# An attention-and-mixer kernel on one core: all work recast as jobs placed by a list scheduler

## The chip, the cores and the metric

The kernel runs on one core of a Trainium2 chip. Its engines are TensorE (PE in the rows, its weight loads PEld), VectorE (DVE), ScalarE (ACT), GpSimd (POOL) and SyncE (SP, which here only issues DMAs). The metric is the device time of one execution, in microseconds (us); lower is better.

## The reference, cut to what matters

The input x has 2048 tokens of 448 features. Two blocks follow each other, both on a normalised input:

```python
h  = x + A(layernorm(x))          # A: attention, 16 heads of 28
h2 = h + B(layernorm(h))          # B: gated mixer over the tokens
# A: qkv = xn @ wqkv; a token attends to the 8 tokens at distances 0, 2, .., 14 behind it
#    logits = q . k * scale; softmax over the 8; o = attn @ v; o @ wo
# B: z = gelu_tanh(hn @ w_in)                 (2048 x 1792)
#    z1 = z[:, :896];  z2 = layernorm(z[:, 896:])
#    g = w_sp @ z2 + b_sp[:, None]            (w_sp is 2048 x 2048)
#    B = (z1 * g) @ w_out
```

## The kernel before, in words

Everything is recorded through `iss`, which puts an instruction into the list of one engine and works out the semaphores that it must wait for. Each engine runs its list in order, and the order is the one in which the code below calls `iss`.

Tokens lie in 16 blocks of 128 (index m). The features, 448, are cut into 4 chunks of 112 rows (`DC`, `NCH`), so a product over the features is 4 matmuls. First x is loaded in four DMAs, with the weights and 16 transposing loads of the upper half of w_sp behind them in SP's list. Layer norm 1: `bn_stats` and `bn_aggr` for each block, one chain of small instructions for the inverse root (`rsqrt_chain`), one `tensor_scalar` for each block (L351). TensorE transposes the normalised block (L360) and VectorE copies it out into `xhT` (L369). Q and K come in tiles of 512 tokens (L383), V for each attention block (L400).

Attention runs in 18 blocks of 114 queries and 128 keys (`NQ`, `PAD`): 16 logit matmuls of 32 rows each, four of which can lie side by side in the array (L416), into banks 0 to 3 of the result memory; four exponentials (L423); one multiplication with the mask of the allowed distances (L432); 16 small matmuls with V, where the weights are the exponentials (L444); a reciprocal and a scaling (L454, L457); a transposition on TensorE (L472) and its copy (L475). `y_block` multiplies with wo and adds x (L485, L488), and L491 takes the squares for layer norm 2. One loop over the slots interleaves these by hand, with the Q, K tiles of later tokens as fillers.

Then the mixer. All layer norm 2 work comes first (16 norms, 64 transpositions). A pipelined loop over 32 half blocks makes z2 (L744). Gelu is built by hand in `GeluTile`: a copy on ScalarE (L708), three products on VectorE (L712 to L714), a sigmoid on ScalarE (L718), a product with a running sum on VectorE (L723), and squares on ScalarE (L733). When all 16 blocks have their sums, L787 normalises z2. The last loop runs over 28 tiles of 128 mixer columns by 512 tokens: 4 matmuls of z1 (L755) and its Gelu, 16 matmuls of w_sp with z2 (L800), bias and gate on VectorE (L813, L815); behind each 7 tiles come 4 blocks of the output product, 7 matmuls each (L823), the residual (L827) and the store (L829).

## Time and profile before

| | |
|---|---|
| time, three runs | 342.18, 343.89, 343.75 us; median 343.75 |
| profiled execution: first to last instruction | 342.4 us |
| mean granted TensorE clock | 0.915 of full speed |
| TensorE busy | 287.6 us (84%), 1859 matmuls |
| VectorE busy | 242.8 us (71%), 670 instructions |
| ScalarE busy | 156.8 us (46%), 320 instructions |
| GpSimd busy | 5.1 us (1%), 17 instructions |
| DMA | 16.39 MB, 40537 packets |

The profile has a time of its own only as the span, 342.4 us; 1.35 us lie between it and the median of the runs. Busy times say how much an engine did, not what the time waited for: that is read from the chain of waits and from the stretches (windows) of the span. A clock of 0.50 means 1.2 GHz, 1.00 means 2.4 GHz.

### The profile page before, as it was taken

To read this page: it belongs to the slowest core of one execution; us is meant where nothing else is said; L and a number is where in the kernel's file an instruction comes from. 1 tells how busy PE (TensorE), PEld (TensorE's weight loads), DVE (VectorE), ACT (ScalarE), POOL (GpSimd) and SP (SyncE) were. 2 spreads that over 40 slices of the span, in tenths; PEclk is the share of its full clock that TensorE was granted. 3 is DMA by queue.
4 is the path that set the end of the run, shared out by engine and by line. 5 is a ranking of instruction groups with operands and counts; after the bars stand their busy time and mean duration, and the time that the engine had idled before them with its cause. 6 is when DMAs were issued, how large, how long until landed. Compare 5 with 4: busy or idle time off the path is not lost.

```text
span 342.4 us, 4998 instructions
## 1 busy us (share of the span) xinstructions
PE 287.6 (84%) x1859; PEld 144.9 (42%) x1872; DVE 242.8 (71%) x670; ACT 156.8 (46%) x320; POOL 5.1 (1%) x17
## 2 busy tenths in 40 slices
PE   3789899999998848966550099999999999999996
PEld 1434455555565617521110034444444444444442
DVE  4987446897779779899999896554555565545554
ACT  1435878777866020899999322221222022212220
POOL 5000000000000000000000000000000000000000
PEclk9879989999987556999996589999999999999999
DMA  7999900000000069930000000001000100000001
GB/s 223 258 220 179 190 16 2 2 0 2 3 2 1 2 162 187 161 76 0 0 1 1 0 2 0 0 2 50 3 3 0 38 17 0 0 26 30 1 0 54
DMA packets 40537, 16.39 MB, mean 48 GB/s; under 512 B 34177, under 2 KB 39617, under 8 KB 40514
## 3 DMA queue, kind: packets, MB, share of 16 engines
q1 hardware_dynamic: 40514, 16.08, 22.5%
q8 instruction: 14, 0.23, 0.3%
q14 instruction: 9, 0.07, 0.1%
HBM read 5.85 MB, written 1.84 MB: 22 GB/s over the span
## 4 chain that ended last, share of the span: by engine, by line
PE 66%; DVE 28%; ACT 2%; issue 2%; DMA 1%; ACTq 0%; DVEq 0%
PE psum L800 29%; PE psum L383 9%; PE psum L755 7%; PE psum L823 6%; DVE z2p L723 5%; PE psum L400 4%; PE psum L485 4%; PE psum L444 4%; DVE wk L714 3%; DVE wk L712 3%; DVE wk L713 3%; DVE xhT L369 2%; DVE tring L351 2%; PE psum L416 2%; DVE st L347 1%
## 5 line engine op out<-in xcount | busy, mean ns | idle before, releaser
L708 ACT ACTIVATE xb<-psum 128x448 bf16<-128x448 f32 (+1 forms) x60 | 33.4, 558 | 108.3 <-PE psum L755 95.5
L800 PE MATMUL psum<-wspT_lo,z2p 128*128 128x512 bf16 x217 | 52.7, 388 | 17.9 <-DVE z2p L787 17.4
L712 DVE TENSOR_TENSOR wk<-xb 128x448 bf16<-128x448 bf16 (+1 forms) x60 | 24.2, 404 | 40.1 <-ACT xb L708 40.1
L800 PE MATMUL psum<-wspT_hi,z2p 128*128 128x512 bf16 x218 | 49.7, 379 | 0.3
L423 ACT ACTIVATE E<-psum 128x456 bf16<-128x456 f32 (+1 forms) x72 | 39.6, 550 | 15.1 <-PE psum L472 8.8
L800 PEld LDWEIGHTS psum<-wspT_lo,z2p 128*128 128x128 bf16 x224 | 21.9, 98 | 46.9 <-DVE z2p L787 22.3
L718 ACT ACTIVATE tb<-wk 128x448 bf16<-128x448 bf16 (+1 forms) x60 | 35.9, 598 | 12.7 <-DVE wk L714 12.7
L744 PE MATMUL psum<-w_in,xhT 112*128 112x448 bf16 x128 | 28.7, 365 | 11.1 <-ACT xb L708 11.1
L800 PEld LDWEIGHTS psum<-wspT_hi,z2p 128*128 128x128 bf16 x224 | 21.9, 98 | 26.5
L755 PE MATMUL psum<-xhT,w_in 112*128 112x512 bf16 x112 | 28.8, 379 | 1.2 <-ACT xb L708 1.2
L714 DVE TENSOR_TENSOR wk<-wk,xb 128x448 bf16<-128x448 bf16 (+1 forms) x60 | 24.5, 408 | 2.1
L744 PEld LDWEIGHTS psum<-w_in,xhT 112*128 112x128 bf16 x128 | 11.4, 101 | 28.0 <-ACT xb L708 19.0
L444 PEld LDWEIGHTS psum<-V,E 128*114 128x114 bf16 (+1 forms) x288 | 21.4, 149 | 2.4 <-issue 0.4
L823 PE MATMUL psum<-w_out,z1p 128*128 128x448 bf16 x112 | 22.0, 353 | 0.1
L444 PE MATMUL psum<-V,E 128*114 128x29 bf16 (+1 forms) x288 | 21.7, 210 | 0.0
L485 PE MATMUL psum<-wo,OT 112*128 112x448 bf16 x64 | 18.4, 420 | 3.9 <-DVE OT L475 2.8
L432 DVE TENSOR_TENSOR E<-E,maskb 128x1824 bf16<-128x1824 bf16 (+1 forms) x18 | 19.9, 1103 | 1.8 <-ACT E L423 1.7
L813 DVE TENSOR_TENSOR ub<-psum,bb 128x512 bf16<-128x512 f32 x28 | 19.1, 683 | 2.3 <-PE psum L800 2.3
L723 DVE CUSTOM_DVE_ANT_0 z2p<-tb,xb 128x448 bf16<-128x448 bf16 x32 | 19.8, 618 | 0.9 <-ACT tb L718 0.8
L383 PE MATMUL psum<-xhT,wqp 112*128 112x512 bf16 x64 | 18.1, 440 | 2.3 <-DVE xhT L369 2.3
L827 DVE TENSOR_TENSOR tring<-psum,x_tm 128x448 bf16<-128x448 f32 x16 | 10.0, 624 | 13.5 <-PE psum L823 13.5
L713 DVE TENSOR_SCALAR wk<-wk 128x448 bf16<-128x448 bf16 (+1 forms) x60 | 17.1, 285 | 2.1
(82 smaller groups left out, 338.1 us busy)
## 6 DMA issues: line engine op xcount, KB each, us to landing
x_tm<-in_A_x_dram SPq DMA_DIRECT2D x4, 448.0 KB, 7.2
out_dram<-tring SPq DMA_DIRECT2D x16, 112.0 KB, 1.7
w_in<-in_B_w_in_dram SPq DMA_DIRECT2D x1, 1568.0 KB, 15.5
stg<-in_A_wqkv_dram SPq DMA_DIRECT2D x1, 1176.0 KB, 9.9
w_out<-in_B_w_out_dram SPq DMA_DIRECT2D x1, 784.0 KB, 4.5
...
wspT_lo<-in_B_w_sp_dram SPq DMA_TRANSPOSE x16, 4.0
wspT_hi<-in_B_w_sp_dram SPq DMA_TRANSPOSE x16, 4.1
```

Of the source, the lines that this page charges most:

```text
L383: e.matmul(out_ap, wsrc[:, c, gg, :], xhT[0:DC, c, col0:col0 + 512], start=(c == 0), stop=(c == NCH - 1)),
L423: iss("act", lambda e, in_ap=in_ap, out_e=out_e: e.activation(out_e, in_ap, AF.Exp, scale=SCALE), reads=[r_bank[hh]], writes=[r_E[slot]])
L444: e.matmul(psum[0:nq, ob + h * 32: ob + h * 32 + DH + 1], E[0:nk, slot, eidx, 0:nq], V1[0:nk, vslot, h, 0:DH + 1]),
L708: iss("act", lambda e: e.activation(self.XB, self.in_ps_ap, AF.Copy), reads=[self.rbank], writes=[r_xb[s]])
L712: iss("dve", lambda e: e.tensor_tensor(self.WK, self.XB, self.XB, ALU.mult), reads=[r_xb[s]], writes=[r_wk[s]])
L714: iss("dve", lambda e: e.tensor_tensor(self.WK, self.WK, self.XB, ALU.mult), reads=[r_wk[s], r_xb[s]], writes=[r_wk[s]])
L718: iss("act", lambda e: e.activation(self.TB, self.WK, AF.Sigmoid, scale=GELU_K2), reads=[r_wk[s]], writes=[r_tb[s]])
L723: iss("dve", lambda e: e.tensor_tensor_reduce(self.out_dst_ap, self.TB, self.XB, 1.0, 0.0, ALU.mult, ALU.add, self.sum_x_ap), reads=[r_tb[ ...
L744: iss("pe", lambda e, c=c: e.matmul(out_ap, xhT[0:DC, c, PAD + 128 * m: PAD + 128 * m + 128], w_in[:, c, FH + D * k: FH + D * (k + 1)], st ...
L755: iss("pe", lambda e, c=c: e.matmul(out_ap, w_in[:, c, fc * 128:(fc + 1) * 128], xhT[0:DC, c, PAD + 512 * tc: PAD + 512 * (tc + 1)], start ...
L800: iss("pe", lambda e, sbk=sbk: e.matmul(out_ap, z2p[:, sbk, fc * 128:(fc + 1) * 128], wsrc[:, sbk, coff:coff + 512], start=(sbk == 0), sto ...
L823: iss("pe", lambda e, fc=fc: e.matmul(out_ap, z1p[:, fc, 128 * m:128 * m + 128], w_out[:, fc, :], start=(fc == 0), stop=(fc == FC7 - 1)), ...
```

## The change

The program is written again. Every piece of work is a `job`: an engine, a key (its rank), a duration written into the source, the instructions, the tiles that it reads and writes, and the banks of the result memory that it takes or gives back. `Planner.order` puts the jobs into one order: of the jobs whose inputs are ready on an engine it takes the lowest key, and one that is ready at once goes before one that is not. Then `Sched.issue` records them with their semaphores as before. What is different in the work:

- Chunks of the features are 128, 128, 128 and 64 rows. The rest of 64 rows is stored twice, in partitions 0 to 63 and 64 to 127, and two matmuls of 64 rows stand behind each other on the two halves of the array. So two tiles take 6 + 2 matmuls in place of 8.
- Two neighbouring banks are taken together, and one instruction empties both: Q and K of one group, two attention blocks of V, half of the heads' exponentials, both halves of z2, two tiles of z1, two blocks of y.
- Attention has 19 blocks of 112 queries; the exponentials as weights are 128 columns wide (they overlap the next head's).
- The transpositions of the normalised blocks 4 to 15, of the 19 attention outputs and of the 16 norms of h are DMAs from SBUF to SBUF (`dma_T`, 47 in all). Blocks 0 to 3 still go through TensorE. GpSimd copies the last 64 columns, so that the transposition also makes the second copy of the rest.
- The normalised blocks go through a ring of 6 (`xn`, `NR`), the attention outputs through one of 3 (`otm`, `NO`).
- The inverse roots are taken for two blocks at a time, 8 instructions on VectorE for blocks 0 to 3, 10 on GpSimd for all others.
- Gelu is one ScalarE instruction. The layer norms of h and of z2 use `bn_stats`, block by block, so there is no barrier over all blocks.
- b_sp is loaded already broadcast, 128 copies of 4 KB. The mixer's first product starts when the last logits are done (`gate`), z2 before z1 before g.

The core of the difference:

```diff
-NQ = 114
-PAD = 14
-NAB = 18
+NQ = 112
+KEYS = 128
+PAD = 16
+NAB = 19
+NPT = 4
+DMA_RATE = 0.25
+NWARM = 30
+FIRST = [(0, 2), (2, 4), "q", "v", (4, 8), (8, 12), (12, 16), "o"]
...
-        class GeluTile:
...
-                iss("dve", lambda e: e.tensor_tensor(self.WK, self.XB, self.XB, ALU.mult), reads=[r_xb[s]], writes=[r_wk[s]])
-                iss("dve", lambda e: e.tensor_scalar(self.WK, self.WK, GELU_C, 1.0, ALU.mult, ALU.add), reads=[r_wk[s]], writes=[r_wk[s]])
-                iss("dve", lambda e: e.tensor_tensor(self.WK, self.WK, self.XB, ALU.mult), reads=[r_wk[s], r_xb[s]], writes=[r_wk[s]])
...
-                iss("act", lambda e: e.activation(self.TB, self.WK, AF.Sigmoid, scale=GELU_K2), reads=[r_wk[s]], writes=[r_tb[s]])
...
-                    iss("dve", lambda e: e.tensor_tensor_reduce(self.out_dst_ap, self.TB, self.XB, 1.0, 0.0, ALU.mult, ALU.add,
-                                                               self.sum_x_ap),
...
-                iss("act", lambda e: e.activation(junk2[:, 0:self.n], self.out_dst_ap, AF.Square, accum_out=self.sum_sq_ap),
...
-        def ot_block(b):
...
-                iss("pe", lambda e, c=c: e.transpose(psb[0:DC, base + c * 128: base + c * 128 + nq],
-                                                    otm[0:nq, oslot, c * DC:(c + 1) * DC], ident[0:nq, 0:nq]),
...
+    def order(self):
...
+                    late = t > te[e] + 1e-9
+                    k = (late, t if late else 0, j.key, j.idx)
+                    if bestj is None or k < bestj[0]:
+                        bestj = (k, j, t, bk)
+                if bestj is not None and (cand is None or bestj[2] < cand[2]):
...
+        NR = 6
+        xn = sb("xn", [128, NR, 512], BF16)
+        NO = 3
+        otm = sb("otm", [128, NO, 512], BF16)
...
+        for what in FIRST:
+            if what == "v":
+                load_c("wv", wv, A_wqkv[:, 2 * D:3 * D], D, W_v)
+            elif what == "q":
+                load_c("wq", wraw, A_wqkv[:, 0:2 * D], 2 * D, W_qk)
+            elif what == "o":
+                load_c("wo", wo, A_wo, D, r_wo2)
+            else:
+                load_x(*what)
+        load_c("w_in", w_in, B_w_in, 2 * FH, r_wi, key=1.0)
+        load("bb", lambda: bb[:], lambda: B_b_sp.rearrange("(o n) -> o n", o=1).to_broadcast([128, S_TOK]), [r_bb], 0.48, 0, key=1.05, mb=0.5)
...
+        def ln_norm(k, m, mv, src3, rsrc, key, dup):
+            s = ringc[0] % NR
+            ringc[0] += 1
+            mu, rstd = mv[:, m, 0:1], rs[k][:, 3, m:m + 1]
+            pl.job("n%d_%d" % (k, m), "dve", key,
+                   [(lambda e: e.tensor_scalar(xn[:, s, 0:D], src3[:, m, :], mu, rstd, ALU.subtract, ALU.mult),
+                     [rsrc, r_mv[k][m], r_rs[k][m]], [r_xn[s]])], dve_t(D, 4, 2))
+            if dup:
+                pl.job("nd%d_%d" % (k, m), "pool", key,
+                       [(lambda e: e.tensor_copy(xn[:, s, D:512], xn[:, s, 384:D]), [r_xn[s]], [r_xnd[s]])], 0.34)
+            return s
+
...
+        def dma_T(name, dst, src, reads, writes, key):
+            return load(name, dst, src, writes, 1.15, 1.5, key=key, transpose=True, reads=reads)
...
+                def f(e, lo=lo, hi=hi, n=n, g=g, tk=tk):
+                    for k in range(2):
+                        for c in range(3):
+                            e.matmul(psv(tk, k, n), wap(0, 128, c, 2 * g + k), xhT[:, c, PAD + lo:PAD + hi],
+                                     start=(c == 0), stop=False)
+                    for k in range(2):
+                        ins = e.matmul(psv(tk, k, n), wap(64 * k, 64, 3, 2 * g + k),
+                                       xhT[64 * k:64 * k + 64, 3, PAD + lo:PAD + hi],
+                                       start=False, stop=True, tile_position=(64 * k, 0))
+                    return ins
+                pl.job("qk%d_%d" % (t, g), "pe", key, [(f, r_pad[2 * g:2 * g + 2] + xh_res(lo, hi), [])], pe_t(*([n] * 7)) + 0.1, acq=tk)
...
+                lgs[(b, j)] = pl.job("lg%d_%d" % (b, j), "pe", b + 0.0, [(f, rq, [])], 0.24, acq=tk, after=[o_jobs.get(b - NE)])
...
+            dma_T("oT%d" % b, lambda t0=t0, nq=nq: OT[:, :, t0:t0 + nq], lambda os=os, nq=nq: otm[0:nq, os, :],
+                  [r_otm[os], r_otd[os]], [r_OT[b]], b + 1.0)
...
+        gate = [lgs[(NAB - 1, 1)]]
...
+            pl.job("z2_%d" % m, "pe", ZK + m, [(f, r_wi + [r_hn[m]], [])], pe_t(*([D] * 7)) + 0.1, acq=tk, after=gate)
+            pl.job("z2g%d" % m, "act", ZK + m,
+                   [(lambda e, m=m, tk=tk: e.activation(
+                       z2p[:, m, :].rearrange("p (k n) -> p k n", k=2),
+                       psum[:, tk.b * 512:tk.b * 512 + 1024].rearrange("p (k n) -> p k n", k=2)[:, :, 0:D],
...
+            load("wlo%d" % s, lambda dst=dst, s=s: dst[:, s % 8, :], lambda s=s: B_w_sp[0:1024, 128 * s:128 * s + 128],
+                 [r_wlo[s]], 1.24, 1.9, key=3.0 + 1.0 * s, transpose=True)
...
+                    pl.job("g%d_%d_%d" % (fc, tc, q), "pe", GK + gi + 0.01 * q, [(f, rw + [r_z2[s] for s in ss], [])],
+                           pe_t(*([512] * 4)), acq=tk if q == 0 else None, use=[tk], reserve=4 if gi < 7 else 0)
...
+                pl.job("ua%d_%d" % (fc, tc), "dve", GK + gi,
+                       [(lambda e, tc=tc, s=s, tk=tk: e.scalar_tensor_tensor(ub[:, s, :], psv(tk), 1.0 / 16.0, bb[:, 512 * tc:512 * tc + 512], ALU.mult, ALU.add),
+                         [r_bb], [r_ub[s]])], dve_t(512), use=[tk], rel=tk)
...
```

SP's list from its start, in the kernel before. `stg` is wqkv, `wspT_lo` the transposed upper half of w_sp:

```order
L296 DMA x_tm<-in_A_x_dram 128x4x448 x2
L302 DMA stg<-in_A_wqkv_dram 112x4x1344
L296 DMA x_tm<-in_A_x_dram 128x4x448 x2
L305 DMA wo<-in_A_wo_dram 112x4x448
L306 DMA w_in<-in_B_w_in_dram 112x4x1792
L307 DMA bsp<-in_B_b_sp_dram 1x2048
L309 DMA_TRANSPOSE wspT_lo<-in_B_w_sp_dram 128x1024 x16
L666 DMA w_out<-in_B_w_out_dram 128x7x448
```

And in the changed kernel, from the load of w_in on. `wsp_la` is the first half of the same, `xhT` takes the transposed norms of x, `OT` the attention outputs; a wait names the engine, and none on these rows waits for an earlier DMA:

```order
L455 DMA w_in<-in_B_w_in_dram 128x3x1792
L455 DMA w_in<-in_B_w_in_dram 64x1792 x2
L455 DMA bb<-in_B_b_sp_dram 128x2048
L454 DMA_TRANSPOSE wsp_la<-in_B_w_sp_dram 128x1024 x8
L454 DMA_TRANSPOSE xhT<-xn 128x4x128 [waits sem_pool,sem_dve] x4
L455 DMA w_out<-in_B_w_out_dram 128x7x448
L454 DMA_TRANSPOSE xhT<-xn 128x4x128 [waits sem_pool] x4
L454 DMA_TRANSPOSE OT<-otm 128x4x112 [waits sem_pool] x2
L454 DMA_TRANSPOSE xhT<-xn 128x4x128 [waits sem_pool] x3
```

The transposed norms of blocks 4 to 7 now stand behind all first loads and eight transposing loads of w_sp; before, TensorE made them and SP had no part in it.

VectorE's list at the first attention blocks, in the kernel before:

```order
L351 TENSOR_SCALAR tring<-x_tm,mv,rst 128x448 x8
L369 COPY xhT<-psum 112x4x128 x2
L432 TENSOR_TENSOR E<-E,maskb 128x1824
L369 COPY xhT<-psum 112x4x128 x2
L432 TENSOR_TENSOR E<-E,maskb 128x1824
L454 RECIPROCAL rcp<-psum 114x16
L457 TENSOR_TENSOR otm<-psum,rcp 114x448
L432 TENSOR_TENSOR E<-E,maskb 128x1824
```

And in the changed kernel. `sem_q26` to `sem_q29` are the DMAs that transpose blocks 4 to 7, `sem_q31` and `sem_q32` those of blocks 8 and 9; L564 writes the norms of blocks 10 to 15 here:

```order
L737 TENSOR_TENSOR E<-E,maskb 128x1792 [waits sem_act]
L564 TENSOR_SCALAR xn<-x_tm,mv_61,rs_66 128x448 [waits sem_q26,sem_pool]
L564 TENSOR_SCALAR xn<-x_tm,mv_61,rs_66 128x448 [waits sem_q27]
L754 RECIPROCAL rcp<-psum 112x16 [waits sem_pe]
L737 TENSOR_TENSOR E<-E,maskb 128x1792 [waits sem_act]
L757 TENSOR_TENSOR otm<-psum,rcp 112x448 [waits sem_dve]
L737 TENSOR_TENSOR E<-E,maskb 128x1792 [waits sem_act]
L754 RECIPROCAL rcp<-psum 112x16 [waits sem_pe]
L564 TENSOR_SCALAR xn<-x_tm,mv_61,rs_66 128x448 [waits sem_q28,sem_pool]
L757 TENSOR_TENSOR otm<-psum,rcp 112x448 [waits sem_dve]
L564 TENSOR_SCALAR xn<-x_tm,mv_61,rs_66 128x448 [waits sem_q29]
L564 TENSOR_SCALAR xn<-x_tm,mv_61,rs_66 128x448 [waits sem_q31,sem_pool]
```

The norm of block 10, which reuses the ring's slot of block 4, now stands behind the first mask and waits for a DMA; the second mask stands behind it.

TensorE's list where attention ends, in the kernel before (L472 transposes an attention output, L485 is y, L360 transposes the norms of h, L744 is z2, L800 is g):

```order
L444 MATMUL psum<-V,E 110x29 x16
L485 MATMUL psum<-wo,OT 128x448 x4
L472 MATMUL psum<-ident,otm 112x110 x4
L485 MATMUL psum<-wo,OT 128x448 x4
L680 MATMUL psum<-bsp,ones 128x512 x4
L360 MATMUL psum<-ident,tring 112x128 x64
L744 MATMUL psum<-w_in,xhT 128x448 x128
L755 MATMUL psum<-xhT,w_in 128x512 x8
L800 MATMUL psum<-wspT_lo,z2p 128x512 x16
```

And in the changed kernel, from the last logits on (L721; their last block has 32 queries). L746 is the product with V, L780 and L783 are y, L811 and L814 z2:

```order
L721 MATMUL psum<-qkT 48x32 x16
L746 MATMUL psum<-V_78,E 128x29 x16
L780 MATMUL psum<-wo,OT 128x448 x6
L783 MATMUL psum<-wo,OT 128x448 x2
L811 MATMUL psum<-w_in,hnT 128x448 x6
L814 MATMUL psum<-w_in,hnT 128x448 x2
L746 MATMUL psum<-V_78,E 128x29 x16
L811 MATMUL psum<-w_in,hnT 128x448 x6
L814 MATMUL psum<-w_in,hnT 128x448 x2
```

z2 of block 0 now comes 4 rows behind the last logits, among the last attention products, where before it came behind all of y and all transpositions. Its 28 tiles of g stand behind all of z2 and z1.

## Rows read from the trace of the kernel before

**Rows 1.** Windows by stage: us; busy us (instructions) by engine; PEclk; DMA share; GB/s.

```profile
0.00:18.50 18.50, 9.44 (x44) 4.67 (x45) 13.17 (x45) 5.12 (x9) 5.06 (x17) 0.91 0.94 243
18.50:127.00 108.50, 98.44 (x964) 57.53 (x964) 79.81 (x212) 68.31 (x126) 0.00 (x0) 0.86 0.28 55
127.00:195.00 68.00, 37.10 (x200) 18.05 (x200) 63.00 (x215) 53.12 (x131) 0.00 (x0) 0.85 0.35 58
195.00:334.00 139.00, 137.08 (x624) 62.21 (x638) 83.20 (x195) 30.28 (x54) 0.00 (x0) 0.98 0.03 11
334.00:342.40 8.40, 5.52 (x29) 2.46 (x26) 3.62 (x6) 0.00 (x0) 0.00 (x0) 1.00 0.16 55
```

**Rows 2.** The chain of waits, last stage: start us, us, what.

```profile
300.24 3.46 PE psum L800 x16
303.70 5.30 PE psum L823 x28
...
334.08 0.70 DVE ub L813
...
339.67 0.62 DVE tring L827
```

**Rows 3.** Timeline of the start: start us, us, engine, line, operation, tiles, count, idle before.

```profile
4.16 0.63 DVE L347 BATCH_NORM_STATS2 st<-x_tm 128x6 f32<-128x448 bf16 x1 [4.16 <-DMA x_tm<-in_A_x_dram]
...
5.03 0.63 DVE L347 BATCH_NORM_STATS2 st<-x_tm 128x6 f32<-128x448 bf16 x1
...
11.25 0.17 DVE L232 TENSOR_SCALAR rsa<-mv 128x8 f32<-128x8 f32 x1
...
14.49 2.54 DVE L351 TENSOR_SCALAR tring<-x_tm,mv,rst 128x448 bf16<-128x448 bf16 x8
...
18.50 1.87 PE L383 MATMUL psum<-xhT,wqp 112*128 112x512 bf16 x4 [1.72 <-DVE xhT L369]
```

**Rows 4.** The page's part 2: GB/s in 40 slices of 8.56 us.

```profile
GB/s 223 258 220 179 190 16 2 2 0 2 3 2 1 2 162 187 161 76 0 0 1 1 0 2 0 0 2 50 3 3 0 38 17 0 0 26 30 1 0 54
```

**Rows 5.** SP: first two transposing loads (timeline), then all 16 (min/median/max ns), and landing.

```profile
10.85 10.91 SPq L309 DMA_TRANSPOSE wspT_lo<-in_B_w_sp_dram  x2
L309 SPq DMA_TRANSPOSE wspT_lo<-in_B_w_sp_dram x16: 1298/1301/5924, 10.9 to 40.2; - x16
DMA to landing us min/median/max: 3.6/4.0/12.0
```

**Rows 6.** Groups by line and form: busy us, mean ns of one; idle before.

```profile
L423 ACT ACTIVATE E<-psum 128x456 bf16<-128x456 f32 x68 | 37.5, 551 | 13.8 <-PE psum L472 8.8 <-PE psum L416 0.2 <-PE psum L444 0.2
L432 DVE TENSOR_TENSOR E<-E,maskb 128x1824 bf16<-128x1824 bf16 x17 | 18.8, 1105 | 1.8 <-ACT E L423 1.7
L457 DVE TENSOR_TENSOR otm<-psum,rcp 114x448 bf16<-114x448 f32 x17 | 10.6, 624 | 0.6
L488 DVE CUSTOM_DVE_ANT_0 x_tm<-psum,x_tm 128x448 bf16<-128x448 f32 x16 | 9.9, 621 | 6.3 <-PE psum L485 6.3
L454 DVE RECIPROCAL rcp<-psum 114x16 f32<-114x16 f32 x17 | 4.4, 256 | 8.8 <-PE psum L444 8.7
```

**Rows 7.** Windows around a pause of TensorE (columns as in rows 1).

```profile
124.00:130.00 6.00, 2.25 (x21) 2.25 (x22) 5.45 (x25) 1.10 (x2) 0.00 (x0) 0.50 1.07 269
130.00:136.00 6.00, 4.51 (x48) 4.06 (x47) 6.00 (x20) 0.00 (x0) 0.00 (x0) 0.78 1.11 189
```

**Rows 8.** Timeline of TensorE in one attention block.

```profile
89.45 0.38 PE L416 MATMUL psum<-qT,kT 32*128 32x114 bf16 x16
89.76 0.41 PE L472 MATMUL psum<-ident,otm 114*112 114x114 bf16 x4
90.01 0.55 PE L444 MATMUL psum<-V,E 128*114 128x29 bf16 x8
```

**Rows 9.** Timeline of GpSimd: two dependent small instructions.

```profile
2.19 0.29 POOL L318 TENSOR_SCALAR_AFFINE_SELECT mf<-mf 128x128 f32<-128x128 f32 x1
2.55 0.29 POOL L320 TENSOR_SCALAR_AFFINE_SELECT mf<-mf 128x128 f32<-128x128 f32 x1
```

More of the change, by code (lines that the diff above doesn't have):

```diff
@@ L9 @@
 DH = 28
-F_DIM = 1792
 FH = 896
@@ L122, in emit, with __init__ @@
                 continue
-            ins = fn(eng)
-            if prod is not None:
-                ins.then_inc(sems[prod], inc)
+            fn(eng).then_inc(sems[prod], inc)
+class Ticket:
+    __slots__ = ("n", "b", "res")
+    def __init__(self, n):
+        self.n = n
+        self.b = None
+        self.res = Res("ticket")
+class Job:
+    __slots__ = ("eng", "key", "dur", "lat", "ops", "acq", "rel", "tick", "reserve",
+                 "deps", "ndep", "succ", "idx", "start", "end", "name", "tbl", "mb")
@@ new lines, in spot @@
+        def spot(name, lo, n, gen=0):
+            r = Res(name, lo, lo + n)
+            r.over = [p for p, g in placed if g < gen and p.lo < r.hi and r.lo < p.hi]
+            placed.append((r, gen))
+            return r
+        x_tm = sb("x_tm", [128, NB, D], BF16)
+        hnT = sb("hnT", [128, 4, S_TOK], BF16)
+        w_in = sb("w_in", [128, 4, 2 * FH], BF16)
+        wo = sb("wo", [128, 4, D], BF16)
+        wsp_la = sb("wsp_la", [128, 8, 1024], BF16)
+        bb = sb("bb", [128, S_TOK], BF16)
@@ new lines, in bass_sequential_preLN__sliding_local_dilated__mixer_gmlp__prompt_kernel, with load, f @@
+        nload = [0]
+        def load(name, dst, src, writes, dur, lat, key=None, transpose=False, reads=(), after=(), mb=0.0):
+            def f(e):
+                if transpose:
+                    return e.dma_start(dst(), src(), transpose=True)
+                return e.dma_start(dst(), src())
+            nload[0] += 1
+            return pl.job(name, "sp", nload[0] * 0.001 - 50 if key is None else key,
+                          [(f, list(reads), list(writes), True)], dur, lat, after=after, mb=mb)
@@ new lines, in bass_sequential_preLN__sliding_local_dilated__mixer_gmlp__prompt_kernel @@
+        for i in range(NWARM):
+            tk = Ticket(1) if i == 0 else tk
+            pl.job("warm%d" % i, "pe", -100.0 + i,
+                   [(lambda e, tk=tk: e.matmul(psv(tk), ident[:], warm[:], start=True, stop=True), [r_ident, r_warm], [])],
+                   0.25, acq=tk if i == 0 else None, use=[tk], rel=tk if i == NWARM - 1 else None)
+        ordered = pl.order()
+        for j in ordered:
+            brs = []
+            for t in j.tick:
+                brs += r_bank[t.b:t.b + t.n]
+            for op in j.ops:
+                fn, reads, writes = op[0], list(op[1]), list(op[2])
+                if j.eng == "pe":
+                    writes += brs
+                else:
+                    reads += brs
+                key = sch.issue(j.eng, fn, reads, writes, dma=len(op) > 3)
+                if j.name.startswith("out"):
+                    sch.store_keys.append(key)
```

1258 lines of the change are left out of this document (614 added, 644 removed).

## The prediction

> **What bounds the kernel now.** I read the windows first, one for each stage [rows 1]. The reader is to see four stages with four limits. In the first 18.5 us TensorE waits for the first normalised blocks. In attention (108.5 us) TensorE is busy 98.4 us, but its clock is 0.86 and part of that is transposition. In the z2 stage (68 us) it is busy only 37.1 us, and VectorE 63.0: the Gelu built by hand is the limit. In the last stage (139 us) it is busy 137.1 us at a clock of 0.98. Then the chain of waits: in the last stage it runs on TensorE alone, 3.46 us for each 16 matmuls of g and 5.30 us for 28 of the output product, so 216 ns for 512 columns and 189 ns for 448, at the full clock [rows 2]. Behind the last g come bias, gate, 28 matmuls, a residual and a store, 8.3 us from 334.08 to the end [rows 1, 2]. So the g products and the output (448 x 0.216 + 112 x 0.189 = 96.8 + 21.2 = 118 us) stay as they are. What can be won lies ahead of them.
>
> I build the new time forward from rows of before: when the last logits are done, since the mixer starts there, then TensorE's work behind them.
>
> **The start.** VectorE begins on x at 4.2 us and needs 0.875 us for one block's statistics [rows 3]. Four blocks: 7.7 us. The chain of inverse roots before is 16 small instructions in 3.24 us, 0.20 each [rows 3]; the new one is two of 8, interleaved: 10.9 us. Four norms at 2.54 / 8 = 0.32 us [rows 3], and a copy: about 13 us, where the first product of Q stood at 18.5 us [rows 3]. On VectorE twelve more statistics follow (10.5 us) and norms 4 to 9 (1.9), so the first mask is done at about 26.5 us.
>
> **The first wait that it adds.** VectorE's next instruction is the norm of block 10. It reuses the ring slot of block 4, so it waits until SP's DMA has transposed block 4. Behind it in VectorE's list stand masks 1 and 2 and all that follows; behind those, on TensorE, the attention products. When does this DMA land? Ahead of it in SP's list stand all first loads: x 1.84 MB, wqkv 1.20, wo 0.40, w_in 1.61, the broadcast b_sp 0.52, together 5.57 MB, and eight transposing loads of w_sp, 0.26 MB each: 7.67 MB. In the kernel before the queue moved 223, 258, 220, 179 and 190 GB/s in its first five slices of 8.56 us [rows 4], which adds up to 7.53 MB at 34.2 us. There the first two transposing loads held SP for 10.9 us while 5 MB of loads drained ahead of them, and the others took 1.30 us each [rows 5]. So block 4 (0.13 MB) lands at about 36.5 us and block 7 at 34.2 + (8.19 - 7.53) / 0.19 = 37.7, and 38.5 with something for completion. VectorE stands still from 26.5 to 36.5 us, TensorE too.
>
> Q and K of tokens 512 to 1023 need blocks 4 to 7, and the fifth attention block (number 4) needs them. Four jobs of 7 x 0.216 = 1.5 us are 6.1 us. After the pause I expect a low clock: before, a stretch in which TensorE was busy 2.25 of 6 us had 0.50, and the next one, with 4.5 busy, 0.78 [rows 7]. At 0.50 it is 12.1 us; I take 8.5, so 47 us. Logits are 0.31 us a block [rows 8]; an exponential of 456 columns takes 0.551 us [rows 6], so two of 896 at most 2.2 us. For blocks 3 and 4 in a row that gives mask 4 at 51.3 us. Masks 1 and 2, the scalings and the norms 10 to 15 fit in between.
>
> **Attention from there.** It is VectorE's list that I expect to bind, from mask 4 to the scaling ahead of the last logits. 12 masks at 1.105 us are 13.3. 12 reciprocals and scalings, 0.256 + 0.624, are 10.6. 5 additions of y, each two of the 0.621 us kind in one, 6.2 [rows 6]. 10 statistics at 0.875 are 8.8, 8 norms at 0.32 are 2.6 [rows 3]. Together 41.4 us. ScalarE beside it has 12 x 2.2 us of exponentials and some 15 us for Q, K and V, which is as much, but it starts earlier. New on GpSimd is the inverse root for layer norm 2: 10 instructions, each of which needs the one before. Two such that depend on each other start 0.36 us apart [rows 9], so 3.6 us; the list gives VectorE 2 to 3 us of other work before the norm that waits. I take 3 us for the five pairs. So the last logits are done at 51.3 + 41.4 + 3 + 0.3 = 96 us.
>
> **TensorE behind the last logits.** Three y pairs, 21 x 0.189 = 4.0. Three attention products, 2 x 0.40 each by the starts in a full-clock block (at most 0.55 for 8 [rows 8]): 2.4. z2: 16 x 7 x 0.189 = 21.2. z1: 14 x 7 x 0.216 = 21.2. g and the output, 118.0. Two halves side by side: the logits show 16 matmuls of 32 rows and 114 columns in 0.31 us, 19 ns each, while 114 columns alone are 48 ns at 2.4 GHz, so matmuls on different rows of the array do run together [rows 8]; I count one matmul for two halves, and for the switch 0.1 us a job (bounds: nothing and one more matmul, 0.2), 33 jobs, 3.3. Sum 170.1 us.
>
> Two waits: the last y needs the last attention output through mask, product, scaling, DMA (4 us to landing [rows 5]), and the last z2 needs another such DMA behind it, two statistics and a root on GpSimd, some 13 us; ahead of them stand twelve z2 (17 us) and six z1 (9 us). I take 5 us (bounds 0 and 12). VectorE has about 50 us of work in these 56 and should not bind: 32 half statistics with what belongs to them (22 to 28), 16 norms of at most 0.64 each, and the rest of attention. ScalarE has one instruction for a tile that took three, 30 x 1.1 to 1.2 us, 35: no bound either. The tail behind the last g is 8.3 us, of which 5.3 are counted: 3.0.
>
> Sum: 96 + 170.1 + 5 + 3.0 = 274.1 us of span. Between span and median lie 1.35 us before, which I keep: **275 us**, a fifth less than 343.75. The gain comes from three places: Gelu and the barrier of the z2 stage (its 68 us become some 56 together with z1, which also leaves the last stage), an eighth of the matmuls over the features, and the start.
>
> **Rivals.**
>
> *No wait at the start* (0.12). If the queue let blocks 4 to 7 through early, VectorE would go on at 26.5 us: masks 1 to 3, four scalings and six norms are 8.7 us, mask 4 at 35.6, last logits at 78 with 41.4 and no loss on GpSimd; 78 + 170.1 + 3 + 1.35 = 252 us. Against it: SP's list has no way past the loads, and even at 258 GB/s throughout, 7.8 MB take 30 us.
>
> *Roots on GpSimd hold up VectorE* (0.16). The trace shows no GpSimd work behind 5.6 us, so nothing on how it runs beside VectorE [rows 1]. While VectorE waits nothing can slow GpSimd, so a wait is at most the whole chain, 3.6 us, in place of the 0.6 I took: 5 pairs x 3.0 = 15 us, 290 us. The Trainium skill, GPSIMD Engine Reference, section Specifications, says that the engine shares its SBUF interfaces with VectorE and contends with instructions of two SBUF inputs or in a two-port mode; masks and norms would be such. By that rule this is the case that comes; no run here shows it yet.
>
> *Halves do not overlap* (0.09), so that part of the change does nothing: one more matmul in each of 19 jobs of 448 and 14 of 512 columns behind the logits, 6.6 us less the 3.3 counted, and a little in attention, which VectorE covers: about 279 us. Against it stand the 19 ns [rows 8].
>
> *The SBUF transpositions bind, slower than before* (0.03). SP issues 47 of them, one after the other, t each. 8 transposing loads are out at about 32 us, 19 more come ahead of the last transposition of h (24.7 us at 1.30 [rows 5]), and from there 4 + 2.6 + 9.1 + 118 + 3 + 1.35 = 138 us remain: 195 + 47 t. That is above 345.5 from t = 3.2 us. With the 1.30 of a load of twice the bytes [rows 5] it gives 256, no bound; half of it, by bytes, less. I use 1.3. In the trace a transposing load carries 128 x 1024 numbers, eight blocks of 128 x 128, in 1.30 us [rows 5]. The Trainium skill, VectorE: DVE Perf Modes, section "The three transpose paths", gives 1309 ns for one block of 128 x 128 by DMA and advises TensorE where its result memory will do; this speaks against the change. Taken as a rate, four blocks would be 5.2 us and the time 441 us, an estimate from that section of the Trainium skill; the trace has its figure only as the time of one instruction, not of one block.
>
> **How the numbers follow.** The forecast as worked out has 0.60, and its own range is 264 to 287: 9 us either way for the clock after the pause, the wait at the last y, and the switches. The rivals have 0.12, 0.16, 0.09 and 0.03. The range reaches down to 254, which leaves out most of the first rival, and up to 297, past the second; about 0.15 is left out. About 0.5% (1.7 us) is what a measurement of this kernel can tell from no change. Every case but the last is far below that: faster 0.96, same 0.01, slower 0.03.
>
> **What would show it.** Right: VectorE idle at a norm that waits for a DMA, from about 27 to 36 us; a low clock of TensorE around 30 to 45; from 51 to 95 us VectorE over 90% busy; the first z2 at 96; TensorE without a gap over 2 us from there except ahead of the last y and z2; g from about 153 at 3.46 us for 16. Wrong: the first z2 before 85 or behind 105; norms that wait for GpSimd by more than 1 us each; SBUF transpositions that hold SP for over 2 us each; z2 jobs of 1.5 us and more at the full clock, which would mean that halves follow each other; g tiles that wait for z2.

## The result and the profile after

The changed kernel takes **284.71 us** (median of 4 runs, 284.02 to 286.0) against 342.97 for the kernel before, a ratio of 0.833 with a 95% interval of 0.828 to 0.838. The forecast was 275 us, its range 254 to 297. The profiled execution took 284.85 us, with a span of 283.1: 9.0 us above the 274.1 that the prediction built up. Executions in a slower state (lower clock, time over 1.5% above the fastest of the same kernel) are left out of the ratios and times below, among them one run of the kernel with w_sp, w_in and b_sp behind x and two of the last kernel.

The windows by stage, with the columns of [rows 1]: the start to the first mask, the pause, the way to mask 4, attention to the last logits, products up to the first g, and g with the output.

```profile
0.00:26.80 26.80, 23.81 (x210) 12.58 (x210) 16.74 (x60) 15.59 (x30) 14.32 (x64) 1.00 1.01 257
26.80:34.80 8.00, 0.66 (x20) 0.49 (x16) 0.00 (x0) 2.90 (x4) 0.79 (x5) 0.56 1.08 182
34.80:51.50 16.70, 14.84 (x128) 5.92 (x128) 7.66 (x15) 8.24 (x10) 8.49 (x29) 0.80 0.67 138
51.50:102.70 51.20, 44.81 (x564) 21.59 (x564) 35.81 (x71) 34.83 (x42) 22.86 (x63) 0.97 0.30 52
102.70:160.80 58.10, 56.09 (x316) 21.47 (x314) 40.29 (x98) 30.25 (x33) 27.80 (x130) 0.97 0.71 136
160.80:283.10 122.30, 118.21 (x562) 54.62 (x560) 41.27 (x72) 1.02 (x1) 0.00 (x0) 1.00 0.05 16
```

The second row is the new wait: VectorE does nothing for 8 us, TensorE nearly nothing, the DMA engines are full. The clock in it is 0.56 and in the row behind 0.80. The fourth row shows where the forecast went most astray: in attention VectorE is busy 35.8 of 51.2 us and TensorE 44.8. The stage that had 68 us for z2 alone in [rows 1], with VectorE at 63.0, has become 58.1 us in which TensorE works 56.1 and does z1 as well.

VectorE's timeline around the pause: mask 0, the norm of block 10, mask 1, and then mask 4 (L564 is a norm, L737 a mask; mask n belongs to attention block n, counted from 0):

```profile
25.69 1.09 DVE L737 TENSOR_TENSOR E<-E,maskb 128x1792 bf16<-128x1792 bf16 x1 [1.11 <-ACT E L730]
34.81 0.40 DVE L564 TENSOR_SCALAR xn<-x_tm,mv,rs 128x448 bf16<-128x448 bf16 x1 [8.03 <-DMA xhT<-xn]
...
36.29 1.03 DVE L737 TENSOR_TENSOR E<-E,maskb 128x1792 bf16<-128x1792 bf16 x1
...
51.54 1.09 DVE L737 TENSOR_TENSOR E<-E,maskb 128x1792 bf16<-128x1792 bf16 x1 [0.53 <-ACT E L730]
```

SP's timeline says why: eight transposing loads of w_sp hold it for 18.53 us ahead of the four transpositions of x. The first two took 4.83 and 4.86 us, where [rows 5] has 10.91 for two; five of the others took 1.30 and one 2.04.

```profile
13.38 18.53 SPq L454 DMA_TRANSPOSE wsp_la<-in_B_w_sp_dram  x8
32.02 5.14 SPq L454 DMA_TRANSPOSE xhT<-xn  x4
```

The chain of waits behind the pause, start, us, what. The first V job takes 2.40 us for six matmuls that take 1.31 later, the first Q/K job 2.36 where the next has 1.40: the low clock that [rows 7] had shown.

```profile
35.92 2.40 PE psum L674 x6
...
39.35 2.36 PE psum L643 x6
...
42.04 1.40 PE psum L643 x6
```

Who waited in attention, from 51.5 to 102.7 us (engine, line, releaser: us, times, longest). VectorE's waits come to 15.7 us, 6.7 of them for GpSimd's roots; the longest two rows of TensorE's list are short waits for exponentials.

```profile
DVE xn L564 <- POOL rs L539: 6.7, 4, 2.4
DVE x_tm L788 <- PE psum L783: 5.4, 4, 2.0
DVE E L737 <- ACT E L730: 2.3, 3, 1.2
...
PE psum L721 <- ACT E L730: 2.0, 4, 0.7
PE psum L746 <- ACT E L730: 1.6, 3, 0.5
```

TensorE between two z2 jobs and two z1 jobs, at the full clock:

```profile
148.91 1.31 PE L811 MATMUL psum<-w_in,hnT 128*128 128x448 bf16 x6
150.15 0.36 PE L814 MATMUL psum<-w_in,hnT 64*128 64x448 bf16 x2
150.44 1.47 PE L852 MATMUL psum<-hnT,w_in 128*128 128x512 bf16 x6
...
152.17 1.47 PE L852 MATMUL psum<-hnT,w_in 128*128 128x512 bf16 x6
153.57 0.39 PE L855 MATMUL psum<-hnT,w_in 64*128 64x512 bf16 x2
153.89 1.47 PE L852 MATMUL psum<-hnT,w_in 128*128 128x512 bf16 x6
```

From start to start a z2 job is 150.44 - 148.91 = 1.53 us and a z1 job 153.89 - 152.17 = 1.72. Eight whole matmuls at the 0.189 and 0.216 of [rows 2] would be 1.51 and 1.73. The halves have gained nothing.

Where the time went can be read from mask 4, the last logits and the first z2 on the two spans. Three lines of the kernel before, then two of the kernel after:

```profile
56.33 1.11 DVE L432 TENSOR_TENSOR E<-E,maskb 128x1824 bf16<-128x1824 bf16 x1
107.31 0.67 PE L416 MATMUL psum<-qT,kT 32*124 32x110 bf16 x16
135.58 12.88 PE L744 MATMUL psum<-w_in,xhT 112*128 112x448 bf16 x60
...
102.46 0.27 PE L721 MATMUL psum<-qkT 28*48 28x32 bf16 x8 [0.47 <-ACT E L730]
106.11 1.35 PE L811 MATMUL psum<-w_in,hnT 128*128 128x448 bf16 x6
```

The spans differ by 59.3 us. The last logits come only 5.2 us earlier (107.98 to 102.73), about what mask 4 has already (4.8). The first z2 stood 27.6 us behind the last logits and now stands 3.4 behind them, since the rest of attention and its output products no longer go ahead of all of z2: 24.2 us. From the first z2 to the end it is 177.0 us in place of 206.8, 29.8 us less, though the last three pairs of y now stand in that part.

### The profile page after: what moved, and what is told of

Its sections match the earlier page's. It is cut to its first block, busy times and chain, and to the rows that moved or that the text cites. A ratio compares the mean times of both kernels' runs of the same rounds, so it can differ in the third digit from the quotient of the medians.

```text
span 283.1 us, 4554 instructions
## 1 busy us (share of the span) xinstructions
PE 258.4 (91%) x1790; PEld 116.7 (41%) x1790; DVE 141.8 (50%) x314; ACT 92.8 (33%) x116; POOL 74.3 (26%) x289
## 4 chain that ended last, share of the span: by engine, by line
PE 62%; SPq 14%; DVE 8%; POOL 6%; DMA 5%; issue 3%; ACT 1%
PE psum L898 34%; SPq L454 10%; PE psum L919 8%; PE psum L643 6%; SPq L455 4%; PE psum L674 3%; PE psum L852 3%; DMA OT<-otm 3%; PE psum L780 2%; DVE x_tm L788 2%; POOL rs L532 2%; DVE st L545 2%; PE psum L746 1%; PE psum L646 1%; DMA hnT<-xn 1%
## 5 line engine op out<-in xcount | busy, mean ns | idle before, releaser
L907 DVE SCALAR_TENSOR_TENSOR ub<-psum,bb 128x512 bf16<-128x512 f32 x28 | 19.4, 692 | 71.0 <-PE psum L898 71.0
L898 PE MATMUL psum<-wsp_hi,z2p 128*128 128x512 bf16 x224 | 48.8, 379 | 0.0
L730 ACT ACTIVATE E<-psum 128x896 bf16<-128x896 f32 (+1 forms) x38 | 30.9, 914 | 6.8 <-PE psum L721 6.8
L898 PEld LDWEIGHTS psum<-wsp_hi,z2p 128*128 128x128 bf16 x224 | 21.9, 98 | 26.3
L898 PE MATMUL psum<-wsp_la,z2p 128*128 128x512 bf16 x112 | 26.5, 379 | 0.0
L898 PE MATMUL psum<-wsp_lb,z2p 128*128 128x512 bf16 x112 | 26.5, 379 | 0.0
L643 PE MATMUL psum<-xhT,wqk 128*128 128x512 bf16 (+2 forms) x144 | 26.1, 319 | 0.0
L564 DVE TENSOR_SCALAR xn<-x_tm,mv,rs 128x448 bf16<-128x448 bf16 x32 | 11.5, 396 | 24.0 <-POOL rs L539 15.3
L811 PE MATMUL psum<-w_in,hnT 128*128 128x448 bf16 x96 | 20.9, 354 | 1.9 <-ACT z1p L871 1.2
L652 ACT ACTIVATE qkT<-psum 128x1024 bf16<-128x1024 f32 (+2 forms) x24 | 17.6, 739 | 13.4 <-PE psum L646 13.3
L737 DVE TENSOR_TENSOR E<-E,maskb 128x1792 bf16<-128x1792 bf16 (+1 forms) x19 | 19.6, 1031 | 4.7 <-ACT E L730 4.7
L852 PE MATMUL psum<-hnT,w_in 128*128 128x512 bf16 x84 | 20.6, 381 | 0.0
## 6 DMA issues: line engine op xcount, KB each, us to landing
bb<-in_B_b_sp_dram SPq DMA_DIRECT2D x1, 512.0 KB, 10.6
```

The source lines that it names most:

```text
L643: e.matmul(psv(tk, k, n), wap(0, 128, c, 2 * g + k), xhT[:, c, PAD + lo:PAD + hi], start=(c == 0), stop=False)
L730: return e.activation(o, i, AF.Exp, scale=SCALE / 256.0)
L737: return e.tensor_tensor(a, a, maskb[0:nk, mi:mi + 1, 0:nq].to_broadcast([nk, NHEAD, nq]), ALU.mult)
L811: e.matmul(psv(tk, k, D), hnT[:, c, cc:cc + 128], w_in[:, c, FH + D * k:FH + D * (k + 1)], start=(c == 0), stop=False)
L852: e.matmul(psv(tk, i), w_in[:, c, 128 * fc:128 * fc + 128], hnT[:, c, 512 * tc:512 * tc + 512], start=(c == 0), stop=False)
L898: ins = e.matmul(psv(tk), z2p[:, s, 128 * fc:128 * fc + 128], w[:, 512 * (tc % 2):512 * (tc % 2) + 512], start=(s == 0), stop=(s == NB - 1))
```

## The experiments

The first loads did not end at the same time in all executions: among the four kernels whose lists are the same up to mask 4 (the kernel after, halves alternate, roots on VectorE, root in one step) mask 1 stands between 36.3 and 37.3 us and mask 4 between 51.5 and 54.5. So stretches tell more than totals here; the table has them in us, from VectorE's and TensorE's timelines of each profiled execution.

| kernel | mask 4 at | to last logits | to first g | to the end | ratio to before (95%) |
|---|---|---|---|---|---|
| the kernel after | 51.5 | 51.2 | 58.1 | 122.3 | 0.833 (0.828 to 0.838) |
| w_sp behind x | 41.3 | 53.6 | 58.7 | 122.4 | 0.813 (0.807 to 0.819) |
| w_sp, w_in, b_sp behind x | 46.7 | 53.1 | 58.4 | 122.3 | 0.820 (0.810 to 0.830) |
| own places for norms | 51.7 | 52.2 | 58.6 | 122.3 | 0.841 (0.836 to 0.845) |
| blocks 4 to 7 on TensorE | 49.9 | 52.5 | 58.0 | 122.3 | 0.828 (0.825 to 0.831) |
| no halves | 55.5 | 51.1 | 59.9 | 122.3 | 0.842 (0.835 to 0.850) |
| halves alternate | 53.7 | 52.4 | 57.7 | 122.3 | 0.837 (0.831 to 0.843) |
| roots on VectorE | 54.5 | 53.5 | 57.8 | 122.3 | 0.841 (0.833 to 0.848) |
| less work for TensorE | 48.6 | 51.6 | 59.0 | 122.3 | 0.836 (0.831 to 0.841) |
| root in one step | 52.6 | 49.4 | 58.1 | 122.3 | 0.838 (0.830 to 0.846) |

**How much is Gelu?** The kernel before, with Gelu in one instruction:

```
-  copy, x*x, scale and add, times x, sigmoid, times x     (2 ScalarE, 4 VectorE)
+  activation(out_dst, in_ps, AF.Gelu_apprx_tanh, accum_out=sum_x)
```

> The kernel before with one thing changed: Gelu is one instruction of ScalarE on the result memory, with the sum that the layer norm needs, in place of a copy, a sigmoid and four operations of VectorE; squares stay on ScalarE. It tells how much of the 58 us Gelu alone brings. Theory (the built Gelu sets the z2 stage, 63 us of VectorE in 68): VectorE has 32 x 1.9 us less, the stage is set by ScalarE with 32 x 1.2 = 37 us or so behind norms and transpositions of the first half (some 6 us), 68 becomes 42 to 48 us, the last stage as it is (TensorE sets it): time 320 to 326. Rival (the barrier, norms and transpositions set the stage): 335 or more.

Measured: 323.42 us, ratio 0.944 (0.938 to 0.949). Theory right for the time: 20 of the 58 us are Gelu's. It was wrong for the stage, which came down to 54 us, not to 42 to 48. Windows of that kernel's z2 stage, and what is left in it on TensorE's timeline:

```profile
126.00:180.00 54.00, 38.98 (x211) 19.04 (x210) 19.51 (x67) 35.84 (x130) 0.00 (x0) 0.87 0.40 68
174.52 6.31 PE L789 MATMUL psum<-wspT_lo,z2p 128*128 128x512 bf16 x15 [12.05 <-DVE z2p L776]
```

VectorE falls from 63.0 to 19.5 us, but TensorE still stands 12.05 us at the barrier where all z2 must be normalised before the first g. From its first z2 to the end this kernel takes 320.9 - 133.1 = 187.8 us, so Gelu gives 19.0 of the 29.8 us of that part. How the other 38 us divide no run shows; by the two spans above most of them, 24.2, lie between the last logits and the first z2.

**What makes the wait at the start?** Four kernels. First, the transposing loads of w_sp behind block 7 of x:

```
-  load("wlo%d" % s, ..., transpose=True)
+  load("wlo%d" % s, ..., transpose=True, after=[xTd[7]])
```

> Edit: the sixteen transposing loads of w_sp may be placed only behind the transposition of block 7 of x, so the eight that stood ahead of blocks 4 to 7 on SP (26.3 us of SP's time up to 32 us) now stand behind. Theory (SP's order makes the wait at the start): the other 5.6 MB of first loads are through at about 24 us, blocks 4 to 7 are transposed by about 26 us, the 8.0 us in which VectorE waits at the norm of block 10 become under 1 us, and the time falls by 7 to 11 us, to 274 to 278. Rival (the pause is covered: attention is set by GpSimd's roots and by TensorE, which catch up): the wait at the start goes and the last logits still come at about 100 us; the time falls by 3 us at most, to 282 or more.

Measured: 278.33 us, 6.4 below the kernel after (7.1 by the spans), intervals apart. SP's timeline: the four transpositions of x now stand at 19.66.

```profile
19.66 5.66 SPq L454 DMA_TRANSPOSE xhT<-xn  x4
25.38 2.75 SPq L454 DMA_TRANSPOSE wsp_la<-in_B_w_sp_dram  x2
```

The time is just above the 274 to 278 of the theory and far from the 282 of the rival. Theory right for the start: mask 4 is 10.2 us earlier. Of that, 7.1 us arrived at the end: attention got 2.4 us longer and what follows 0.7. Then the loads of w_in and b_sp moved as well:

```
-  load_c("w_in", ..., key=1.0)
+  load_c("w_in", ..., key=1.0, after=[xTd[7]])        (b_sp alike)
```

> As the run before, and the loads of w_in (1.61 MB) and of the broadcast b_sp (0.52 MB) are placed behind block 7 of x too. Theory (SP's order and the bytes ahead make the wait): blocks 4 to 7 land at about 20 to 23 us, no wait of VectorE is left there, mask 4 comes at about 40 us instead of 51.5, and the time is 1 to 4 us below that of the run before, 271 to 276. Rival (only the transposing loads held SP): no difference from the run before.

Measured: 281.4 us; theory wrong, and no gain over the run before (the intervals overlap). SP's timeline:

```profile
19.83 5.24 SPq L454 DMA_TRANSPOSE xhT<-xn  x4
25.12 1.75 SPq L455 DMA_DIRECT2D w_in<-in_B_w_in_dram  x3
26.91 0.59 SPq L455 DMA_DIRECT2D bb<-in_B_b_sp_dram  x1
27.54 7.81 SPq L454 DMA_TRANSPOSE wsp_la<-in_B_w_sp_dram  x2
35.39 1.26 SPq L454 DMA_TRANSPOSE OT<-otm  x1
```

Blocks 4 to 7 came no earlier, so the bytes of w_in had not held them. But now two transposing loads stand directly behind 2 MB of plain loads and hold SP for 7.81 us; the next transposition of x stands behind them, and VectorE waited 5.24 and 4.82 us for such. The wait had moved. So it did where TensorE transposes blocks 4 to 7:

```
-NPT = 4
+NPT = 8
```

> Edit: blocks 4 to 7 of x are transposed by TensorE like blocks 0 to 3, not by SP's DMA; so nothing of tokens 512 to 1023 stands behind the loads. Theory (the queue makes the wait at the start): no wait of VectorE at block 10, mask 4 at about 38 to 42 us, time 273 to 278, against 4 x 0.6 us more for TensorE and 4 copies for ScalarE. Rival (pause covered by later waits): time 282 or more. It also tells what SP's order still costs when compared with the runs that only move loads.

Measured: 284.35 us, the rival's time; but the pause is not covered by other waits, as the rival had it. VectorE's timeline shows the same wait one mask later, for a later block that SP transposes behind the same loads.

```profile
38.59 0.40 DVE L564 TENSOR_SCALAR xn<-x_tm,mv,rs 128x448 bf16<-128x448 bf16 x1 [7.97 <-DMA xhT<-xn]
```

Last, the ring: each norm of x in a place of its own.

```
-  s = ringc[0] % NR; write xn[:, s, 0:D]
+  if k == 0: write z2p[:, m, 0:D]      (unused until the mixer)
```

> Edit: the norm of each block of x has a place of its own in the still unused z2p, so that the norm of block 10 doesn't wait for the transposition of block 4; SP's order stays. Theory (the transposition of blocks 4 to 7 comes too late by itself; the ring is only the first to feel it): VectorE works on to its list's next need, mask 4 stays at 50 to 51.5 us, the time is within 2 us of 284.7. Rival (the ring makes the loss: VectorE's 8 us of work lie idle behind it): VectorE does masks 1 to 3 and norms in the pause, mask 4 at 45 us or earlier, time 277 to 280.

Measured: 288.19 us, mask 4 at 51.69. Masks 1 and 2 are done in the pause, at 28.25 and 29.73, and then VectorE waits for TensorE, which waits 8.3 us for transposed blocks of x:

```profile
39.73 0.26 DVE L759 RECIPROCAL rcp<-psum 112x16 f32<-112x16 f32 x1 [8.93 <-PE psum L751]
36.27 2.40 PE L679 MATMUL psum<-wv,xhT 128*128 128x448 bf16 x6 [8.30 <-DMA xhT<-z2p]
```

Theory right for the cause: the ring only felt it first. The time is 3.5 us above the kernel after, more than the 2 allowed (the intervals just overlap), with stretches within 1.0 us of its stretches.

**Do the halves gain?** First without them:

```
-  two matmuls over rows 0:64 and 64:128, tile_position=(64 * k, 0)
+  two matmuls over 128 rows, zeros in rows 64:128 of the weights
```

> Edit: the rest of 64 rows is taken by full matmuls of 128 rows, with zeros in the second copy of the weights, so each pair of products has 8 full matmuls in place of 6 and two halves, and the array is never switched between whole and halves; the output is the same. Theory (the switches eat what the halves win: 1.535 us for a z2 job against 8 x 0.189 = 1.51, 1.72 for a z1 job against 8 x 0.216 = 1.73): jobs within 0.03 us of those, time within 2 us of 284.7. Rival (halves save nearly a whole matmul, and the 0.3 us for two of them is something that full matmuls would pay too): a z2 job 1.70, a z1 job 1.93; 16 x 0.17 + 14 x 0.21 = 5.7 us behind the last logits and 2 to 5 in attention, time 291 to 296.

Measured: 288.01 us; job by job the theory holds, 149.09 - 147.58 = 1.51 and 150.82 - 149.09 = 1.73 us:

```profile
147.58 1.30 PE L807 MATMUL psum<-w_in,hnT 128*128 128x448 bf16 x6
...
149.09 1.46 PE L847 MATMUL psum<-hnT,w_in 128*128 128x512 bf16 x6
...
150.82 1.46 PE L847 MATMUL psum<-hnT,w_in 128*128 128x512 bf16 x6
```

The total is 3.3 us higher, outside the 2 us though the intervals overlap. Mask 4 came 4 us late in it, attention was as long as in the kernel after, and the stretch behind it 1.8 us longer: there one more job ran at the low clock (2.81 us for 1.51) and the waits are 2.3 us in place of 2.0. So it isn't the jobs. Mask 4 came late in another order: the planner put a Q/K job first behind the pause, which needs all of blocks 4 to 7, where the kernel after has a V job, which could go when block 5 had landed. TensorE waited 14.08 us there in place of 7.94. Then half the switches:

```
+  h1 = m % 2 == 1          (every second job: its halves first)
```

> Edit: every second z2 and z1 job takes its two halves first, not last, so that two neighbours have their halves back to back and a job has one switch between whole array and halves in place of two. Theory (each switch costs 0.106 us): the mean job gets 0.106 us shorter, z2 1.43 and z1 1.61 where neighbours follow, 30 x 0.106 = 3.2 us at most, time 281.5 to 283. Rival (the 0.3 us are the halves themselves, one after the other, not the switch): jobs as before, time 284 to 286.

Measured: 288.25 us; theory wrong for the total, which is no lower than that of the kernel after (the intervals overlap). In the jobs the gain is there:

```profile
133.03 2.76 PE L868 MATMUL psum<-hnT,w_in 128*128 128x512 bf16 x12
135.73 0.61 PE L860 MATMUL psum<-hnT,w_in 64*128 64x512 bf16 x4
136.26 2.76 PE L868 MATMUL psum<-hnT,w_in 128*128 128x512 bf16 x12
...
143.54 2.40 PE L821 MATMUL psum<-w_in,hnT 128*128 128x448 bf16 x6 [2.57 <-DMA hnT<-xn]
```

Two z1 jobs take 136.26 - 133.03 = 3.23 us where they took 3.44: two switches fewer, 0.105 us each. What is left of a z1 job, 1.72 - 6 x 0.216 - 2 x 0.105 = 0.21 us, is one whole matmul for both halves. So halves do run side by side, and two switches cost what they save. The stretch behind the last logits is only 0.4 us shorter (57.7 for 58.1). The last row shows where gain was lost: TensorE came to the last z2 jobs earlier and waited for the DMA of h, 2.57 us, and then ran a job at the low clock (2.40 for 1.31).

**What sets attention?** Three kernels take one suspect away each. The roots on VectorE:

```
-  ln_rstd(1, m, 2, mv2, "pool", key + 0.1)
+  ln_rstd(1, m, 2, mv2, "dve", key + 0.1)
```

> Edit: the inverse roots for layer norm 2 (eight chains of ten small operations) on VectorE instead of GpSimd. Theory (the roots on GpSimd hold up VectorE, and attention with it): the waits of VectorE for GpSimd in attention, 6.7 us in 4 norms, go; VectorE gets 8 x 10 operations of 0.2 us at most, and has 15 us of idle time in attention for them; the last logits come 3 to 6 us earlier, the time is 279 to 282. Rival (TensorE sets attention: busy 44.8 of 51.2 us there, and VectorE's wait only takes the place of another): last logits within 1.5 us of 102.5, time 283.5 to 286.

Measured: 287.3 us. VectorE no longer waits for GpSimd, but its work in attention is 43.9 us in place of 35.8, and attention is 53.5 us, not shorter. The theory of the wait fails here, and the rival's times are passed too; as the roots were added to VectorE's work, the wait needs a cleaner test, the root in one step below. Then less work for TensorE:

```
-  6 whole matmuls and two halves for Q, K, V and y
+  6 whole matmuls      (the last 64 features are left out)
```

> Edit: the matmuls over the last 64 features (the two halves) are left out of the products for Q, K and V and of the output projection of attention, so those features don't count there; the order of all instructions stays. Between mask 4 and the last logits that takes 8 x 0.32 + 10 x 0.30 = 5.6 us from TensorE's 44.8. Theory (TensorE's work sets attention, not VectorE's): that stretch falls from 51.2 us to 45.5 to 47.5, and the start and the y products take 3 to 4 us more off; time 274 to 278. Rival (the chain of exponential, mask, sum, statistics and roots sets it): the stretch stays above 49.5 us, TensorE waits more, time 280 or more.

Measured: 285.62 us, and attention 51.6. TensorE has 5.1 us less to do and the stretch is as long. The theory that it sets attention falls too:

```profile
48.60:100.20 51.60, 39.72 (x544) 22.09 (x534) 35.82 (x71) 34.86 (x41) 22.97 (x61) 0.90 0.27 55
PE psum L771 <- DMA OT<-otm: 3.9, 2, 3.8
PE psum L737 <- DVE E L728: 2.9, 2, 1.6
```

It waits longer for the transposed output and for masks, and its clock falls to 0.90. Last, each root of layer norm 2 as a single GpSimd step that leaves out the root itself, with all orders as they were:

```
-  ten dependent operations
+  tensor_single_scalar(rs[k][:, 3, m:m + n], var, EPS, ALU.add)
```

> Edit: the inverse root of the second layer norm is one GpSimd operation in place of ten (so that layer norm has wrong factors); the order of every engine's other instructions is that of the kernel after. It takes the chain of 3.0 to 3.6 us between statistics and norm away and puts nothing on VectorE. Theory (statistics, root, norm, mask is the chain that sets attention: VectorE waited 6.7 us in four norms, with masks queued behind): those waits go, mask 4 to last logits falls from 51.2 to 45 to 48 us, time 278 to 282. Rival (no single link sets it: take one away and the next in the lists waits, as with less work for TensorE, 51.6, and roots on VectorE, 53.5): the stretch stays at 49.5 to 51.5 us, time 283 to 287.

Measured: 286.34 us, attention 49.4 us: the rival, to 0.1 us. GpSimd's waits are gone without new work for VectorE, and the stretch is 1.8 us shorter. ScalarE's timeline:

```profile
67.27 1.02 ACT L656 ACTIVATE qkT<-psum 128x1024 bf16<-128x1024 f32 x1 [2.23 <-PE psum L650]
68.19 3.34 ACT L734 ACTIVATE E<-psum 128x896 bf16<-128x896 f32 x4
```

Exponentials come in bursts here, four in 3.34 us, and the chain of waits runs through them. Summed by engine over attention, pieces of the chain of waits are: in the kernel after TensorE 32.3, VectorE 8.2, GpSimd 5.4, ScalarE 2.7, DMA 2.4 us; with the one-step root TensorE 33.3, ScalarE 13.4, DMA 2.4, VectorE 1.1; with less work for TensorE, TensorE 15.9, VectorE 16.8, GpSimd 10.6, DMA 4.8, ScalarE 1.7. The length is 49.4 to 51.6 in all three. So neither TensorE's work nor the roots on GpSimd alone set attention. The reading that fits is that the lists are fixed, four Q/K jobs in a row leave ScalarE idle, the exponentials behind them leave TensorE idle, and what is taken from one link is waited for at the next; no run changed the order of the lists alone to show it.

**Better kernels.** Two combine edits with the moved loads.

```
-  0.26 * len(ops)
+  0.36 * len(ops)      (planner's price of small GpSimd operations; and halves alternate)
```

> The transposing loads behind block 7 of x, halves alternately first, and the planner is told 0.36 us for each small GpSimd operation in place of 0.26 (the trace has 0.28 to 0.30 from start to start, and 0.94 to 1.14 where a mask runs beside it), so that it places the norms that wait for roots later in VectorE's list, behind masks. Theory (VectorE's waits for GpSimd in attention, 6.7 us in 4, put masks late and with them TensorE): these waits fall below 2 us, and attention from mask 4 to the last logits from 53.6 to 49 to 51; time 274 to 276. Rival (TensorE sets attention, as where the roots went to VectorE and nothing was gained): 277 to 279.5, attention 52 to 54 us.

Measured: 276.61 us, ratio 0.811 (0.807 to 0.815): the fastest, below both the kernel before and the kernel after, but not to be told from the moved loads alone. The time lies between the two forecasts. VectorE's waits for roots in attention are gone, as the theory wanted, but attention did not get shorter: 43.0 to 98.6 us, with one y job more in it and TensorE's clock at 0.88.

```
-  ln_rstd(0, m, n, mv1, "dve" if m < NPT else "pool", key)
+  ln_rstd(0, m, n, mv1, "dve", key)      (and halves alternate)
```

> Three edits on the kernel after: the transposing loads of w_sp behind block 7 of x (278.33 us alone), the inverse roots of the first layer norm on VectorE for all blocks, not on GpSimd from block 4 on, and halves alternately first. Theory (with the loads out of the way, GpSimd's chains of roots, 3.0 us each and one behind the other, time blocks 4 to 15: VectorE waited 2.3, 0.7, 2.0 and 2.2 us for them ahead of mask 4): mask 4 comes at 37 to 39 us in place of 41.3, and attention and what follows are as long as before; time 273 to 276. Rival (the pieces behind fill it again: order of y and QK, last transposition of h): mask 4 earlier, last logits not, time 277 to 280.

Measured: 282.67 us (two runs), ratio 0.828 (0.820 to 0.837): above both expectations and above the moved loads alone, and the interval overlaps that of the kernel after. Why it gives back part of what the moved loads alone had won was not settled.

## Why the prediction was right, and where it was not

*The start, right.* First mask done at 26.5 forecast, 26.78 measured; the norm of block 10 at 36.5, and it came at 34.81, the queue having moved 203, 331 and 305 GB/s in its first slices where [rows 4] had 223, 258 and 220; the four Q/K jobs done at 47, measured 47.21; mask 4 at 51.3, measured 51.54. The mechanism (SP's list has no way past the loads) is shown by the run that moved them. The rival *No wait at the start*, with mask 4 at 35.6 and 252 us, was too cheap even for that order: 41.3 and 278.33.

*Attention, wrong.* The step that failed is "It is VectorE's list that I expect to bind", with its 41.4 us, 3 for the roots and 0.3: 44.7 forecast, 51.2 measured. VectorE had 35.8 us of work, not 41.4, and waited 15.7; it was 70% busy where "over 90%" was to show the forecast right. The part that failed is the overlap: the waits were put at 3 us. I had added up one engine and compared it with one other; TensorE's share, 44.8 us, was not summed at all. But the larger of the two would not have been the answer either, as the three runs show. Two of the prediction's own signs of being wrong came here: the first z2 at 106.1 (forecast 96, the limit 105), and norms that wait for GpSimd by more than 1 us each. That the time still falls within 4% of the forecast is because attention is the only large miss. The rival *Roots on GpSimd hold up VectorE* had its waits in the trace, but in attention they are 6.7 us in four norms, not 15, the longest 2.4 (over the whole run 15.3 in ten norms, those of the start among them). Without them attention is 1.8 us shorter: they lay beside other waits.

*Behind the last logits, right within 1 us, by two errors that cancel.* Forecast 52.1 of work and 5 of waits, measured 56.1 and 2.0. The switch that I took at 0.1 us a job is twice 0.105; over the 33 jobs that is 3.6 us more. The sign that I had given for it, "z2 jobs of 1.5 us and more", came, but not the meaning that I gave it: the halves do not follow each other. The Trainium skill, TensorEngine Tiling (Array Packing), section Key Properties, says that a change of tiling mode drains TensorE; it has no price there, and these rows give 0.105 us. Of the three places named for the gain, "an eighth of the matmuls over the features" gave nothing, and the start gave 4.8 us by mask 4. A place that the list leaves out gave up to 24.2: z2 begins 3.4 us behind the last logits in place of 27.6.

*The last stage*, 121.0 forecast with its tail, 122.3 measured.

*SBUF transpositions, right.* SP was held 1.26 us (median) by each, against 1.30 for a load of twice the bytes, and they landed after 2.4 to 2.5 us where [rows 5] has 4.0. The figure of the Trainium skill, VectorE: DVE Perf Modes, section "The three transpose paths", is therefore that of an instruction: four blocks cost no more here than it gives for one.

The sum: 0.2 at mask 4, 6.5 in attention, 1.0 behind it, 1.3 at the end are the 9.0 us.
